# Fused attention, gated MoE and soft-MoE kernel: the last block and the tail of TensorE in written order, serial stages in column halves, six more weight tiles

## The chip, the cores and the metric

The kernel is one program on one core of one Trainium2 chip. The metric is the device time of one execution in microseconds; the figure for the kernel is the median of several runs. A profile is one more execution, taken with the hardware profiler; its span runs from the first to the last instruction of the core.

## The reference

Three parts, each fed by the one before. Sizes: 8 x 8 heads of 576 tokens by 64; 4608 tokens of width 512; a feed-forward width of 2048; 8 experts with 4 slots each and an inner width of 1024.

```python
# chunked attention, chunks of 64 tokens (q_c, k_c, v_c: the inputs cut into chunks)
scores = scale * np.matmul(q_c, k_c.transpose(0, 1, 2, 4, 3))
attn = softmax over the last axis of scores
x = np.matmul(attn, v_c)                    # as 4608 x 512
# gated layer
h = x @ w_in
g = h * (1.0 / (1.0 + np.exp(-1.702 * h)))
x = g @ w_out
# soft mixture of experts, 32 slots
logits = x @ phi
d = np.exp(logits - logits.max(0, keepdims=True)); d /= d.sum(0, keepdims=True) + 1e-09
slot_input = (d.T @ x).reshape(E, S_per_e, D)
for e in range(E):
    slot_out[e] = np.maximum(slot_input[e] @ w1[e], 0.0) @ w2[e]
c = np.exp(logits - logits.max(1, keepdims=True)); c /= c.sum(1, keepdims=True) + 1e-09
out = c @ slot_out.reshape(n_slots, D)
```

(The softmax is written in one line here; the reference subtracts the maximum and divides by the sum with 1e-9 added.)

## The kernel before

**Blocks.** The 4608 tokens are 12 blocks of 384. In a block the gated layer runs over 16 column tiles `f` of 128 columns of the inner width. `gemm` does one of them: twelve full-width matmuls (`h`, lines 324 to 326; the fp32 product is put together from high and low parts), a tanh on ScalarE, and on VectorE the product that gives the gate tile `gt`. `x @ w_out` is never formed: `logits` multiplies the gates by `wp`, a product of `w_out` and `phi` made ahead, in quarter-width matmuls (32 of the 128 columns of the array each) for four column tiles at a time, and `dispatch` sums the gates into the 32 slots (`dtg`, 12 quarter-width matmuls of 512 columns, added to `acc`). The softmax over the tokens is carried from block to block (`slots_a`, factor `cr`), that over the slots stands in `slots_b`. What `dispatch` needs of the gates is their transpose. The other blocks get it by way of DMA; in the last block `gemm_t` transposes on TensorE, three 128x128 transposes per column tile into an accumulator tile `gtp`, copied out by VectorE or ScalarE (`EVAC` says which), one column behind `gemm`. The work of the block before (its last logits `l3`, `slots_a` as `s0`, `slots_b` as `s1`, its `dispatch` as `d0`) and the logits of the last block itself (`l0` to `l2`) are hung on columns by the list `LAST`.

**The tail.** Behind the last column come the last logits, the softmax (`slots_a`), and a chain on TensorE: `dtg` for the last block; four transposes of `acc` (`accp`), copied by ScalarE to `ac`; 16 quarter-width matmuls with `w_out` (`sip`), scaled by VectorE to `si`; four matmuls with the selection matrix `sel` that transpose and sum (`sitp`), spread by VectorE into `sxt`. Then eight up steps `(g, a)`: 32 quarter-width matmuls or more with `w1` (`h1p`), a ReLU on ScalarE (`h1`), two transposes (`htp`), a copy by VectorE (`ht`). Then the down stage for each half `d` of the 512 output columns: for each half `g` of the experts 32 matmuls with `w2` (`fp`), a copy by ScalarE (`f`), and a matmul that sums over experts (`so`). `combine` multiplies by the slot softmax and stores, the first half on the queue of GpSimd (POOL), the second on that of SyncE (SP).

**Order.** Up to the block before the last all engines run in the order in which the code is written. For the last block and the tail only SP does (line 900); there a scheduler puts the instructions of the other engines in order by their dependences and its own estimate.

**Loads of expert weights.** `w1` and `w2` lie packed in one array and are read in the order of use. `load(kind, eng)` fills one tile of a pool: `w`, `s`, `q`, `v`, `x` and `p` are kinds of tile, and `ROOM` says how many 128 KB pieces one holds. `TABLE` hangs loads on columns of blocks 9 to 11 and on three places of the tail (`a`, `b`, `e`); `used` issues a load into a tile when its pieces have been multiplied. These loads are issued on POOL's queue (line 599).

## Time and profile before

| | |
|---|---|
| median of 3 runs | 648.03 us (647.84 to 648.07) |
| the profiled execution | 645.9 us, span 644.1 us, 15618 instructions |
| TensorE busy | 617.8 us, 96% of the span |
| VectorE busy | 450.6 us, 70% |
| ScalarE busy | 233.2 us, 36% |
| GpSimd busy | 68.2 us, 11% |
| moved by DMA | 167.95 MB, mean 261 GB/s |

The profiled execution took 1.8 us more than its span. Busy shares are means over the whole span, and the ends of matmuls are modelled; what a stretch is bound by is read from its own rows.

### The profile page before, as it was taken

Reading aid. Unit: us, or ns where it says so; the run is one execution under the profiler, and the core shown is the slowest. Engines: PE = TensorE matmul, PEld = TensorE weight load, DVE = VectorE, ACT = ScalarE, POOL = GpSimd, SP = SyncE. Lnnn points to the kernel's source line nnn. Section 1 sums busy time; section 2 is a strip of 40 time slices with the busy share of each in tenths; the row PEclk is TensorE's granted clock in tenths of the full one; section 3 lists DMA queues with packets and bytes.
Section 4 is the critical chain, followed back from the end, with each engine's and each line's share of the span. In section 5 each row is a group of like instructions: output and inputs, shape, how many; then the busy total and the mean of one; then the engine's idle time right before and its main releaser. Section 6 shows DMA issues by size and latency. Waiting matters only on the chain.

```text
span 644.1 us, 15618 instructions
## 1 busy us (share of the span) xinstructions
PE 617.8 (96%) x6476; PEld 525.1 (82%) x6476; DVE 450.6 (70%) x981; ACT 233.2 (36%) x481; POOL 68.2 (11%) x101
## 2 busy tenths in 40 slices
PE   8899999999999999999999999999999999978893
PEld 7699887897898798989889989989898898826552
DVE  5899889788697787786886886877857646331033
ACT  4876454342232343333324333433333222121132
POOL 1000010101010010000000010100001111232310
PEclk9999999999999999999999999999999999999997
DMA  8964885559799794785774966956748789889997
GB/s 338 358 197 192 272 283 167 133 156 337 191 346 285 236 341 138 219 306 165 259 258 147 338 200 169 371 136 200 267 122 285 240 285 380 305 297 415 406 395 297
DMA packets 64503, 167.95 MB, mean 261 GB/s; under 512 B 11888, under 2 KB 34544, under 8 KB 64432
## 3 DMA queue, kind: packets, MB, share of 16 engines
q1 hardware_dynamic: 55824, 129.72, 60.6%
q0 software_dynamic: 8608, 37.23, 15.2%
q8 instruction: 51, 0.84, 0.5%
q14 instruction: 20, 0.16, 0.1%
HBM read 122.29 MB, written 44.63 MB: 259 GB/s over the span
## 4 chain that ended last, share of the span: by engine, by line
PE 91%; DVE 4%; ACT 2%; issue 1%; POOL 0%; DVEq 0%; ACTq 0%; POOLq 0%
PE h L324 21%; PE h L326 20%; PE h L325 20%; PE lp L390 5%; PE dtg L526 5%; PE sx L248 3%; PE sx L299 3%; PE pt L284 2%; PE fp L708 2%; PE h1p L688 2%; PE op L737 1%; PE wpp L200 1%; PE gtp L375 1%; PE sip L652 1%; PE htp L697 1%
## 5 line engine op out<-in xcount | busy, mean ns | idle before, releaser
L324 PE MATMUL h<-xh,w 128*128 128x384 f32 x768 | 265.6, 346 | 0.5 <-ACT xh L314 0.5
L326 PE MATMUL h<-xh,w 128*128 128x384 f32 x768 | 257.6, 335 | 0.5 <-DVE w L187 0.5
L325 PE MATMUL h<-xl,w 128*128 128x384 f32 x768 | 257.3, 335 | 0.0
L328 ACT ACTIVATE gt<-h 128x384 f32<-128x384 f32 x192 | 94.0, 490 | 211.8 <-PE h L326 211.6
L324 PEld LDWEIGHTS h<-xh,w 128*128 128x128 f32 x768 | 144.2, 188 | 20.9 <-issue 16.7
L329 DVE SCALAR_TENSOR_TENSOR gt<-gt,h 128x384 f32<-128x384 f32 x192 | 104.8, 546 | 71.3 <-ACT gt L328 70.9
L326 PEld LDWEIGHTS h<-xh,w 128*128 128x128 f32 x768 | 144.1, 188 | 1.6 <-issue 0.8
L325 PEld LDWEIGHTS h<-xl,w 128*128 128x128 f32 x768 | 144.4, 188 | 0.3 <-DVE xl L315 0.3
L339 DVE STREAM_TRANSPOSE g<-gt 128x384 f32<-128x384 f32 x176 | 100.4, 574 | 7.7 <-PE dtg L526 2.3
L273 POOL TENSOR_TENSOR e<-e,rs 128x512 f32<-128x512 f32 x33 | 34.5, 1046 | 459.3 <-DVE rs L272 418.8
L314 ACT ACTIVATE xh<-sx 128x512 fp32r<-128x512 f32 (+1 forms) x38 | 21.7, 576 | 88.0 <-DVE e L260 76.3
L315 DVE TENSOR_TENSOR xl<-sx,xh 128x512 fp32r<-128x512 f32 (+1 forms) x38 | 24.8, 657 | 20.0 <-ACT xh L314 18.6
L599 POOL DMA_DIRECT2D w<-in_moe_w_dram x56 | 29.8, 534 | 84.1 <-PE h L326 36.8
L390 PE MATMUL lp<-gt,wp 128*32 128x384 f32 x384 | 37.0, 492 | 0.1
L526 PE MATMUL dtg<-g,dt 128*32 128x512 f32 x288 | 33.2, 593 | 1.4 <-DVE dt L485 1.4
L259 DVE TENSOR_REDUCE mx<-sx 128x8 f32<-128x512 f32 (+1 forms) x37 | 23.8, 643 | 6.1 <-PE sx L248 6.1
L260 DVE TENSOR_TENSOR e<-sx,mx 128x512 f32<-128x512 f32 (+1 forms) x37 | 25.0, 677 | 2.3 <-DVE mx L259 0.5
L746 DVE COPY o<-op 128x512 f32<-128x512 f32 (+1 forms) x20 | 11.1, 626 | 21.3 <-PE op L737 21.3
L267 ACT ACTIVATE e<-e 128x512 f32<-128x512 f32 x36 | 22.6, 628 | 7.9 <-DVE e L260 7.8
L526 PEld LDWEIGHTS dtg<-g,dt 128*32 128x32 f32 x288 | 8.9, 110 | 19.8 <-issue 18.2
L269 DVE TENSOR_REDUCE sm<-e 128x8 f32<-128x512 f32 x36 | 23.5, 654 | 0.1
L248 PEld LDWEIGHTS sx<-qk 64*64 64x64 f32 x960 | 16.7, 134 | 7.7 <-issue 7.4
(121 smaller groups left out, 551.0 us busy)
## 6 DMA issues: line engine op xcount, KB each, us to landing
g_dram<-g SPq DMA_DIRECT2D x176, 192.0 KB
g<-g_dram SPq DMA_DIRECT2D x44, 768.0 KB
w<-in_moe_w_dram POOLq DMA_DIRECT2D x34, 512.0 KB, 8.9
qk<-in_qk_dram SPq DMA_DIRECT2D x30, 512.0 KB
w<-in_moe_w_dram POOLq DMA_DIRECT2D x17, 768.0 KB, 7.7
stg<-in_moe_w_in_dram SPq DMA_DIRECT2D x16, 512.0 KB
stg<-in_moe_w_out_t_dram SPq DMA_DIRECT2D x16, 512.0 KB
wo<-in_moe_w_out_dram SPq DMA_DIRECT2D x16, 512.0 KB
```

Of the source, the lines that this page charges most:

```text
L248: nc.tensor.matmul(out=y[h][w, hp, :], lhsT=t[r, 0, hp, w], rhs=t[r, 1, hp, w], start=True, stop=True)
L260: nc.vector.tensor_tensor(out=ev[:, hs], in0=v, in1=mx[:, hs].to_broadcast(list(v.shape)), op=ALU.subtract)
L273: (nc.gpsimd if pool else nc.vector).tensor_tensor(out=e, in0=e, in1=rs.to_broadcast([128, 2 * KD, 64]), op=ALU.mult)
L324: nc.tensor.matmul(out=h, lhsT=a, rhs=xh[b][:, k, :], start=(k == 0), stop=False)
L325: nc.tensor.matmul(out=h, lhsT=a, rhs=xl[b][:, k, :], start=False, stop=False)
L326: nc.tensor.matmul(out=h, lhsT=l, rhs=xh[b][:, k, :], start=False, stop=(k == KD - 1))
L328: nc.scalar.activation(out=t, in_=h, func=ACTF.Tanh, scale=0.851)
L329: nc.vector.scalar_tensor_tensor(out=t, in0=t, scalar=1.0, in1=h, op0=ALU.add, op1=ALU.mult)
L339: nc.vector.transpose(out=g1[b, q][:, :, :, 32 * j:32 * (j + 1)], in_=t.rearrange("p (a b c) -> p b a c", b=4, c=32))
L390: nc.tensor.matmul(out=lp[b][32 * j:32 * (j + 1), :], lhsT=wp[:, f, :], rhs=gt[b, f], start=(g == 0), stop=(g == NG - 1),)
L526: nc.tensor.matmul(out=p[32 * j:32 * (j + 1)], lhsT=dt[:, i, :], rhs=g[j][i], start=(i == 0), stop=(i == NCP - 1))
L599: eng.dma_start(out=t[:, 0:at], in_=w12[:, w_at[0]:w_at[0] + at])
```

## The change

`manual_schedule` now holds TensorE too, so that from the last block on it runs in the order of the code. The code is written for that order: `gemm_t` runs two columns behind `gemm` instead of one (its accumulator tiles come from another pool, tags `x` and `s`), the second group of logits moves from column 12 to column 8, and ScalarE and VectorE change places in the copies of columns 14 and 15. In the tail, `dtg`, `accp`, `sip` and `sitp` are done in halves of 256 columns. An up step (`up`) and its transposes (`turn`) are apart: those of a step are written behind the matmuls of the next. In the down stage (`down`, `total`) the sum of the first half of the experts is written in the middle of the second half's matmuls, and the last step's transposes amid the first `fp`. `slots_b` moves behind `sitp`. The 16 blocks of `w_out` are converted in another order (`wo_use`), so that those which `sip` needs first are neighbours. Six loads of a new kind `m` (tiles of the pool that holds gates and ReLU outputs, two pieces of 128 KB each) are hung on columns 10 to 15 of the last block.

```diff
-ROOM = {'w': 4, 's': 6, 'q': 4, 'v': 2, 'x': 2, 'p': 6}
+ROOM = {'w': 4, 's': 6, 'q': 4, 'v': 2, 'x': 2, 'p': 6, 'm': 2}
 TABLE = {'9.15': 'wxx', '10.6': 'q', '10.11': 'vq', '10.15': 'v', '11.0': 'ssw', '11.8': 'sss', 'a': 'ss', 'b': 'ssss', 'e': 'pppppp'}
 TABLE.update({f'11.{f}': TABLE.get(f'11.{f}', '') + 'w' for f in range(1, 16)})
-EVAC = 'vvvvvvvvvvvvvvaa'
-LAST = (('g0', 2), ('l3', 4), ('l0', 4), ('s0', 5), ('s1', 7), ('d0', 9), ('l1', 12), ('l2', 12))
+TABLE.update({f'11.{f}': TABLE[f'11.{f}'] + 'm' for f in range(10, 16)})
+EVAC = 'vvvvvvvvvvvvvvav'
+LAST = (('g0', 2), ('l3', 4), ('l0', 4), ('s0', 5), ('s1', 7), ('d0', 9), ('l1', 8), ('l2', 12))
...
-        if f % 2:
-            p = ps_x[0].tile([128, NCP, 4, 32], F32, tag="x", name="gtp")
-        else:
-            p = ps.tile([128, NCP, 4, 32], F32, tag="pt", name="gtp")
+        p = ps_x[0].tile([128, NCP, 4, 32], F32, tag="x" if f % 2 else "s", name="gtp")
...
+    wo_use = [j * 4 + g for g in range(4) for j in range(4)]
 
     def load_wo(i):
         if i < NF:
...
+    def m_alloc(shape, dtype, name):
         return mid_tile(shape, name, dtype)
...
+        gemm_t(b, NF - 2)
         logits(b, NG - 1)
         gemm_t(b, NF - 1, gt_last)
...
-        dispatch(b)
-        at("b")
+        dt, cr = dt_t.pop(b)
+        gs = g2.pop(b)
...
+        halves = [(h, slice(256 * h, 256 * h + 256), slice(2 * h, 2 * h + 2)) for h in range(2)]
+        for h, cs, fs in halves:
+            p = ps_h.tile([128, 2, 128], F32, tag="h", name="dtg")
+            for i in range(NCP):
+                for j in reversed(range(4)):
+                    nc.tensor.matmul(
+                        out=p[32 * j:32 * (j + 1)], lhsT=dt[:, i, :], rhs=gs[j][i][:, fs, :],
+                        start=(i == 0), stop=(i == NCP - 1),
+                    )
+            nc.vector.scalar_tensor_tensor(
+                out=acc[:, cs], in0=acc[:, cs], scalar=cr, in1=p.rearrange("p f c -> p (f c)"), op0=ALU.mult, op1=ALU.add
+            )
+        at("b")
+        s = stat[b][1]
+        sip = [ps.tile([128, 256], F32, tag="pt", name="sip"), ps_x[0].tile([128, 256], F32, tag="s", name="sip")]
+        acs = []
+        for h, cs, fs in halves:
+            p = (ps_h if h else ps).tile([128, 2, 4, 32], F32, tag="h" if h else "m", name="accp")
+            for z in range(2):
+                nc.tensor.transpose(
+                    p[:, z].rearrange("p g s -> p (g s)"), acc[:, cs][:, 128 * z:128 * (z + 1)], ident
+                )
+            ac = mid_tile([128, 2, 4, 32], "ac")
+            nc.scalar.activation(out=ac, in_=p, func=ACTF.Copy)
+            acs.append(ac)
+        sums = ps.tile([128, 1], F32, tag="lp", name="sums")
+        nc.tensor.matmul(out=sums, lhsT=sel_all, rhs=s, start=True, stop=True)
+        rs = st_p.tile([128, 1], F32, tag="rsum", name="rsum")
+        nc.vector.scalar_tensor_tensor(out=s, in0=stat[b - 1][1], scalar=cr, in1=sums, op0=ALU.mult, op1=ALU.add)
...
+        sx = []
+        for z in range(2):
+            for h, cs, fs in halves:
+                for g in (2 * z, 2 * z + 1):
+                    for j in range(4):
+                        nc.tensor.matmul(
+                            out=sip[h][32 * j:32 * (j + 1), :], lhsT=acs[z][:, g % 2, j, :], rhs=wo_t[j * 4 + g][:, cs],
+                            start=(g == 0), stop=(g == 3),
+                        )
+        at("e")
+        for h, cs, fs in halves:
+            si = mid_tile([128, 256], "si")
+            nc.vector.tensor_scalar(out=si, in0=sip[h], scalar1=rs, scalar2=0.5, op0=ALU.mult, op1=ALU.mult)
+            p = (ps if h else ps_x[0]).tile([128, 2, NS], F32, tag="m" if h else "x", name="sitp")
+            for k in range(2):
+                nc.tensor.matmul(
+                    out=p[:, k, :], lhsT=si[:, 128 * k:128 * (k + 1)], rhs=sel_all[:, 0:32], start=True, stop=True
+                )
+            x = sxt[h]
+            y = p.rearrange("p k (e i) -> p k e i", i=4)
+            nc.vector.tensor_copy(x[:, :, 0:252].rearrange("p k (e x) -> p k e x", x=36)[:, :, :, 0:4], y[:, :, 0:7])
+            nc.vector.tensor_copy(x[:, :, 252:256], y[:, :, 7])
+            sx += [x[:, 0, :], x[:, 1, :]]
         slots_b(b)
         load_ct(slice(NT // 512 - 1, NT // 512))
...
+        ht, h1 = {}, {}
+
+        def up(g, a):
+            n = 2
...
+            used(*[(1, 4 * g + j, a + z) for j in range(4) for z in range(n)])
+            h1[g, a] = mid_tile([128, n, 128], "h1")
+            nc.scalar.activation(out=h1[g, a], in_=p, func=ACTF.Relu)
+
+        def turn(g, a):
+            n, v = 2, h1.pop((g, a))
+            p = ps.tile([128, n, 128], F32, tag="m", name="htp")
+            if a % 4 == 0:
+                ht[g, "t"] = mid_tile([128, 4, 128], "ht")
+            t = ht[g, "t"]
+            for c in range(n):
+                nc.tensor.transpose(p[:, c, :], v[:, c, :], ident)
+                ht[g, a + c] = t[:, (a + c) % 4, :]
+            nc.vector.tensor_copy(t[:, a % 4:a % 4 + n, :], p)
+
+        steps = [(g, a) for g in range(2) for a in range(0, KE, 2)]
+        for i, x in enumerate(steps):
+            up(*x)
+            if i:
+                turn(*steps[i - 1])
+        so, fp = {}, {}
+
+        def down(d, g, ks):
+            if 0 in ks:
+                fp[d, g] = ps.tile([128, DH], F32, tag="lp" if g else "pt", name="fp")
+            p = fp[d, g]
+            for k in ks:
                 for j in range(4):
-                    c, i = a, 0
-                    while c < a + n:
...
+                    nc.tensor.matmul(
+                        out=p[32 * j:32 * (j + 1), :], lhsT=ht[g, k][:, 32 * j:32 * (j + 1)],
+                        rhs=w2_t[d, 4 * g + j, k], start=(k == 0), stop=(k == KE - 1),
+                    )
...
+            if KE - 1 in ks:
+                f = fp[d, g] = mid_tile([128, DH], "f2")
+                nc.scalar.activation(out=f, in_=p, func=ACTF.Copy)
+
+        def total(d, g):
+            if g == 0:
+                so[d] = ps_x[0].tile([128, DH], F32, tag="x", name="so")
+            nc.tensor.matmul(out=so[d], lhsT=sel_all, rhs=fp.pop((d, g)), start=(g == 0), stop=(g == 1))
+
         for d in range(2):
-            so = ps_x[0].tile([128, DH], F32, tag="x", name="so")
-            for g in range(2):
-                p = ps.tile([128, DH], F32, tag="pt", name="fp")
-                for k in range(KE):
-                    for j in range(4):
-                        nc.tensor.matmul(
-                            out=p[32 * j:32 * (j + 1), :], lhsT=ht[g, k][:, 32 * j:32 * (j + 1)],
-                            rhs=w2_t[d, 4 * g + j, k], start=(k == 0), stop=(k == KE - 1),
-                        )
-                    if k % 4 == 3:
-                        used(*[(2, d, 4 * g + j, k - z) for j in range(4) for z in range(4)])
-                f = mid_tile([128, DH], "f2")
-                nc.scalar.activation(out=f, in_=p, func=ACTF.Copy)
-                nc.tensor.matmul(out=so, lhsT=sel_all, rhs=f, start=(g == 0), stop=(g == 1))
+            down(d, 0, range(4))
+            if d == 0:
+                turn(*steps[-1])
+            down(d, 0, range(4, KE))
+            down(d, 1, range(4))
+            total(d, 0)
+            down(d, 1, range(4, KE))
+            total(d, 1)
             sr = mid_tile([128, DH], "sr")
-            nc.scalar.activation(out=sr, in_=so, func=ACTF.Copy)
+            nc.scalar.activation(out=sr, in_=so[d], func=ACTF.Copy)
             combine(d, sr)
 
...
-            if b == NB - 1 and f:
-                gemm_t(b, f - 1)
+            if b == NB - 1 and f > 1:
+                gemm_t(b, f - 2)
...
-        with tc.manual_schedule(engines={SP}):
+        with tc.manual_schedule(engines={SP, PE}):
             with tc.tile_pool(name="ps_t", bufs=1, space=bass.MemoryType.PSUM) as ps_x[0]:
                 block(NB - 1)
                 tail()
```

The order of instructions on each engine shows what the written order does at two places. The first is TensorE in the last block, behind column 4. `lp_6350` is the last logits group of the block before, the other `lp` is the first group of the last block, `gt_...` are gates (of columns 0 to 3 where `lp` is theirs), `gtp_...` their transposes, and `h_...` with `xh_6336` and `xl_6337` the matmuls of column 5. TensorE before:

```order
L390 MATMUL lp_6350<-gt_6674,wp_89 32x384
L390 MATMUL lp_6816<-gt_6705,wp_89 32x384
L390 MATMUL lp_6816<-gt_6727,wp_89 32x384
L390 MATMUL lp_6816<-gt_6751,wp_89 32x384
L390 MATMUL lp_6816<-gt_6782,wp_89 32x384
L375 MATMUL gtp_6821<-ident_87,gt_6782 128x128 x3
L324 MATMUL h_6828<-xh_6336,w_530 128x384
L375 MATMUL gtp_6731<-ident_87,gt_6705 128x128 x3
L325 MATMUL h_6828<-xl_6337,w_530 128x384
```

The transposes of columns 3 and 0 stand here with matmuls of column 5 between them. TensorE after:

```order
L388 MATMUL lp_6350<-gt_6674,wp_89 32x384
L388 MATMUL lp_6811<-gt_6705,wp_89 32x384
L388 MATMUL lp_6811<-gt_6727,wp_89 32x384
L388 MATMUL lp_6811<-gt_6745,wp_89 32x384
L388 MATMUL lp_6811<-gt_6777,wp_89 32x384
L373 MATMUL gtp_6816<-ident_87,gt_6745 128x128 x3
L325 MATMUL h_6823<-xh_6336,w_530 128x384
L326 MATMUL h_6823<-xl_6337,w_530 128x384
```

Now it is the transposes of column 2, and the matmuls of column 5 follow. Columns 0 and 1 have been transposed earlier.

VectorE at the same place; `lps1` is the subtraction that makes the low part of the block before's logits, and `gtp_6762` (before) and `gtp_6757` (after) are read by the copies of columns 1 and 0. Before:

```order
L379 COPY g2_0_6730<-gtp_6762 128x12x32
L329 SCALAR_TENSOR_TENSOR gt_6751<-gt_6751,h_6738 128x384
L329 SCALAR_TENSOR_TENSOR gt_6782<-gt_6782,h_6769 128x384
L329 SCALAR_TENSOR_TENSOR gt_6805<-gt_6805,h_6792 128x384
L405 TENSOR_TENSOR lps1_6813<-lp_6350,lps0_6812 128x384
L379 COPY g2_0_6730<-gtp_6821 128x12x32
L379 COPY g2_0_6730<-gtp_6731 128x12x32
L379 COPY g2_0_6730<-gtp_6785 128x12x32
```

One of the copies stands ahead of three gates and `lps1`, three behind. After:

```order
L330 SCALAR_TENSOR_TENSOR gt_6777<-gt_6777,h_6764 128x384
L330 SCALAR_TENSOR_TENSOR gt_6800<-gt_6800,h_6787 128x384
L403 TENSOR_TENSOR lps1_6808<-lp_6350,lps0_6807 128x384
L377 COPY g2_0_6756<-gtp_6757 128x12x32
L377 COPY g2_0_6756<-gtp_6780 128x12x32
L377 COPY g2_0_6756<-gtp_6816 128x12x32
```

All three copies stand behind `lps1`, and the first of them, of `gtp_6757`, empties the tile that `gtp_6816` writes on TensorE.

The second place is TensorE in the up steps; `h1p_...` are the matmuls of steps, `h1_7348` (before) and `h1_7388` (after) the ReLU of a step, `htp_...` its transposes. Before:

```order
L688 MATMUL h1p_7319<-w12_6683,sxt_7210 32x128
L688 MATMUL h1p_7319<-w12_6710,sxt_7210 32x128
L688 MATMUL h1p_7354<-w12_6712,sxt_7209 32x256
L688 MATMUL h1p_7354<-w12_6736,sxt_7209 32x256
L688 MATMUL h1p_7354<-w12_6767,sxt_7209 32x256
L697 MATMUL htp_7350<-ident_87,h1_7348 128x128 x2
```

The transposes stand behind three matmuls of the next step. After:

```order
L710 MATMUL h1p_7395<-w12_6785,sxt_7200 32x256
L710 MATMUL h1p_7395<-w12_6712,sxt_7200 32x256
L710 MATMUL h1p_7395<-w12_6730,sxt_7200 32x256
L710 MATMUL h1p_7395<-w12_6762,sxt_7200 32x256
L710 MATMUL h1p_7395<-w12_6785,sxt_7200 32x256
L725 MATMUL htp_7422<-ident_87,h1_7388 128x128 x2
```

They stand behind the last matmul of the next step (`h1p_7395`), ahead of the one after that.

## Rows read from the trace of the kernel before

**Rows 1.** Busy us by stretch: PE, PEld, DVE, ACT, POOL, granted clock, DMA share, GB/s

```profile
549.00:560.00 11.00, 11.00 (x76) 9.64 (x75) 4.82 (x10) 1.97 (x4) 2.83 (x6) 1.00 0.90 340
560.00:571.00 11.00, 9.45 (x70) 5.29 (x68) 4.42 (x15) 3.23 (x9) 2.09 (x4) 1.00 0.83 288
571.00:573.50 2.50, 1.47 (x14) 0.72 (x6) 1.22 (x5) 0.36 (x1) 1.19 (x3) 1.00 0.37 43
573.50:615.00 41.50, 35.94 (x610) 22.63 (x612) 6.80 (x21) 6.34 (x16) 14.14 (x27) 1.00 1.01 403
...
628.00:631.00 3.00, 3.00 (x50) 2.30 (x46) 2.14 (x4) 2.06 (x4) 0.00 (x0) 1.00 0.07 22
```

**Rows 2.** Timeline of PE, serial stages: start, us, instruction [wait ahead, releaser]

```profile
568.72 2.78 PE L526 MATMUL dtg<-g,dt 128*32 128x512 f32 x24 [1.38 <-DVE dt L485]
...
572.45 0.66 PE L637 MATMUL accp<-ident,acc 128*128 128x128 f32 x4 [0.64 <-DVE acc L532]
573.79 3.64 PE L652 MATMUL sip<-wo,ac 128*32 128x512 f32 x32 [0.69 <-ACT ac L639]
578.38 1.08 PE L661 MATMUL sitp<-sel,si 128*128 128x32 f32 x8 [0.95 <-DVE si L658]
579.74 0.40 PE L688 MATMUL h1p<-w,sxt 128*32 128x256 f32 x1 [0.28 <-DVE sxt L668]
```

**Rows 3.** Waits of PE, 579 to 628 us: total us, times, longest

```profile
PE htp L697 <- ACT h L694: 2.0, 6, 0.5
```

**Rows 4.** Timeline of PE, down stage

```profile
605.62 0.70 PE L716 MATMUL so<-f,sel 128*128 128x256 f32 x2 [0.53 <-ACT f L715]
...
621.67 0.70 PE L716 MATMUL so<-f,sel 128*128 128x256 f32 x2 [0.56 <-ACT f L715]
622.30 3.66 PE L708 MATMUL fp<-w,ht 128*32 128x256 f32 x64
```

**Rows 5.** Timeline of DVE, last block

```profile
530.59 0.56 DVE L405 TENSOR_TENSOR lps<-lp,lps 128x384 fp32r<-128x384 f32 x1 [0.26 <-ACT lps L404]
531.16 1.18 DVE L379 COPY g<-gtp 128x384 f32<-128x384 f32 x2
...
564.10 0.55 DVE L329 SCALAR_TENSOR_TENSOR gt<-gt,h 128x384 f32<-128x384 f32 x1 [1.59 <-ACT gt L328]
```

**Rows 6.** Timeline of PE, last block

```profile
530.58 0.55 PE L375 MATMUL gtp<-ident,gt 128*128 128x128 f32 x3
...
560.61 0.33 PE L325 MATMUL h<-xl,w 128*128 128x384 f32 x1
560.79 0.34 PE L326 MATMUL h<-xh,w 128*128 128x384 f32 x1
...
561.47 0.34 PE L325 MATMUL h<-xl,w 128*128 128x384 f32 x1
...
563.38 0.49 PE L375 MATMUL gtp<-ident,gt 128*128 128x128 f32 x3
```

**Rows 7.** Groups by line, 563 to 645 us: busy us, mean ns, idle before

```profile
L532 DVE SCALAR_TENSOR_TENSOR acc<-acc,cr,dtg 128x512 f32<-128x512 f32 x1 | 0.7, 749 | 0.6 <-PE dtg L526 0.6
...
L701 DVE COPY ht<-htp 128x256 f32<-128x256 f32 x8 | 3.4, 425 | 18.3 <-PE htp L697 18.3
...
L694 ACT ACTIVATE h<-h1p 128x256 f32<-128x256 f32 x8 | 3.1, 384 | 24.2 <-PE h1p L688 24.2
```

**Rows 8.** Timeline of PE, up steps

```profile
585.16 1.93 PE L688 MATMUL h1p<-w,sxt 128*32 128x256 f32 x32
587.55 0.44 PE L697 MATMUL htp<-ident,h 128*128 128x128 f32 x2 [0.46 <-ACT h L694]
587.92 1.93 PE L688 MATMUL h1p<-w,sxt 128*32 128x256 f32 x32
```

**Rows 9.** Timeline of POOL: the last load of weights is issued

```profile
608.50 0.54 POOL L599 DMA_DIRECT2D w<-in_moe_w_dram  x1 [0.75 <-DMA w<-in_moe_w_dram]
```

**Rows 10.** DMA issues, 608 to 609.5 us: KB, us from issue to landing

```profile
w<-in_moe_w_dram POOLq DMA_DIRECT2D x1, 256.0 KB, 8.9
```

91 lines of the change are left out of this document (25 added, 66 removed).

## Prediction, made before the changed kernel was run

> **What bounds the kernel now.** I read the busy time by stretch first. From 549 us to 571 us TensorE has hardly a free moment while matmuls of the last block run (11.00 of 11.00 us, then 9.45 of 11.00), so nothing that only hides work there can pay; it pays to take work or waits off TensorE. The same view shows the DMA side: its engines are busy 0.90, 0.83 and 0.37 of the three stretches up to 573.5 us, then 1.01 of a stretch of 41.5 us while the expert weights stream in, and idle (0.07) from 628 to 631 us [rows 1]. The tail is therefore a chain through TensorE beside a full stream of loads, and both have to be followed. The chain of waits and the timeline of TensorE give the chain: four serial stages from 568.72 us to 579.74 us with waits of 0.64, 0.69, 0.95 and 0.28 us on VectorE and ScalarE [rows 2]; eight up steps, each followed by two transposes that wait for the ReLU on ScalarE, 2.0 us in all [rows 3]; and in the down stage sums that wait for a copy by ScalarE [rows 4]. The time behind 628 us is stores.
>
> **The change, part by part.**
>
> *Last block, in written order.* Four things move. (a) The order shows that the transposes of column 2 now stand directly behind eight logits matmuls. They write the accumulator tile that column 0 wrote, which must first be copied out, and on VectorE that copy stands behind the subtraction `lps1`. In the trace before, that subtraction starts at 530.59 us, and the two copies behind it start at 531.16 us and take 1.18 us, so the first ends at about 531.75 us [rows 5]; TensorE came to the place behind the logits at 530.58 us [rows 6]. Before, TensorE had other work whose tile was free. Now it stands: +1.2 us, and behind it in its queue wait the matmuls of column 5, so everything later moves. (b) The logits of columns 4 to 7 are a group of their own, at column 8. The matmuls are the same, but there is one change more from full-width to quarter-width work and back. A change costs about 0.15 us (worked out below): +0.3 us. (c) The transposes of column 13 leave the full stretch and go behind the last matmul of column 15, where TensorE waits for that column's gate anyway. Two matmuls that start 0.17 us apart without transposes start with three of them between at 560.79 us and, two matmuls on, at 561.47 us, so the three cost 0.68 - 0.35 = 0.33 us: -0.3 us. (d) VectorE copies them out before it finishes the gate of column 15. Transposes that start at 563.38 us take 0.49 us [rows 6], a copy 0.56 us (half of the 1.18 us less a little), so VectorE would be free at about 564.4 us; it began the gate at 564.10 us [rows 5]: +0.3 us. Together +1.5 us at 568.72 us. The bounds of (a) are 0 us (the copy comes sooner) and 1.8 us (both copies are waited for).
>
> *Serial stages in halves.* The waits sum to 0.64 + 0.69 + 0.95 + 0.28 = 2.56 us [rows 2]. A copy of 256 columns takes VectorE 0.43 us against 0.75 us for 512, ScalarE 0.38 us [rows 7]. First half: its accumulation on VectorE (0.43 us) lies under the second half of `dtg` (half of 2.78 us). The second half's lies only under the first two transposes (half of 0.66 us), so with 0.15 us of hand-over about 0.25 us stays. ScalarE's first copy (0.38 us) lies under the other two transposes and that wait. The first `si` lies under the last quarter of `sip` (0.9 us), the second under the first half of `sitp` (0.5 us), and the first `sxt` copies under its second half. I keep another 0.2 us for hand-overs. 2.56 - 0.45 = 2.1 us: -2.1 us, bounds 1.5 and 2.5 us. The normalising work of `slots_b` moves behind; on VectorE it stands between the two accumulations in about 0.5 us where the second half is not ready yet, so it costs nothing; without that cover it would cost these 0.5 us.
>
> *Up steps.* Before, the 16 matmuls from 587.92 us are preceded by transposes that started at 587.55 us after 0.46 us of waiting; the period from the matmuls at 585.16 us is 2.76 us [rows 8]. Now the transposes of a step are written behind the whole next step, whose 1.93 us hide the ReLU (0.38 us) [rows 7]. What goes is the waiting, 2.0 us by the view of waits [rows 3]: -2.0 us, bounds 1.6 and 3 us. What does not go is the change between the two kinds of work: matmuls follow 0.37 us after the start of two transposes [rows 8], and two transposes themselves cost 2 x 0.11 = 0.22 us by the 0.33 us for three, so 0.15 us is the change. There are as many of them as before. The Trainium skill, "TensorEngine Tiling (Array Packing)", section Tiling Modes, says that changing the tiling mode drains TensorE. The row agrees (0.15 us). By that rule a sum made from streaming time alone would promise too much: 16 changes of 0.15 us, 2.4 us more.
>
> *Down stage.* The sum of the first half of the slots is now written amid the second half's matmuls, so its wait of 0.53 us in the first pass and 0.56 us in the second goes [rows 4]; those of the second halves stay, since nothing is left to put there: -1.1 us, bounds 0.9 and 1.4 us.
>
> *Loads.* Six loads of 256 KB are issued from column 10 on, behind a load of 512 KB each. They carry 1.57 MB, 3.9 us at the 403 GB/s of the full stretch. Up to 573.5 us the engines are idle for 0.10 x 11 + 0.17 x 11 + 0.63 x 2.5 = 4.5 us [rows 1], so they fit into it, and the stream behind has 3.9 us less to bring. It starts 1.5 us later, with the last block: 2.4 us earlier at its end. The chain does not live on this, since the last load is issued at 608.50 us [rows 9] and lands 8.9 us on [rows 10], at 617.4 us, while the last pass that needs such data starts at 622.30 us [rows 4]; it covers the tail's gain. The stores of the first half end at about 628 - 2.4 = 625.6 us, and those of the second would start at 631 - 3.7 = 627.3 us: no collision, 1.7 us to spare. The order of the `w_out` blocks changes no bytes: 0. The six tiles come out of the pool that also holds the gates and the ReLU outputs; their old contents are last read several columns earlier, so I count no wait.
>
> Sum: +1.5 - 2.1 - 2.0 - 1.1 = -3.7 us, made against a span of 644.1 us (645.9 us with what lies around it). The median of the runs is 648.03 us, 2.1 us above that execution; the same 3.7 us off it gives **644.3 us**.
>
> **The rivals.**
>
> *The changes of mode are hidden too.* If TensorE could begin transposes under the tail of quarter-width matmuls once nothing has to be waited for, the 2.4 us above would go as well: -6.1 us, 641.9 us. Against it: the 0.15 us stands also where nothing was waited for [rows 8].
>
> *The stores bound the end.* If the six loads only push others back, the stream is not 2.4 us earlier but 1.5 us later. First-half stores then end at 629.5 us, second-half ones start there instead of at 631 us, and only 1.5 us come out: 646.5 us. For it: the engines are already busy 0.9 and 0.83 of the time there [rows 1]. Against it: the idle time exceeds the need. The Trainium skill, "DMA: Bandwidth & Descriptors", section Anatomy of one DMA, gives 2.0 us plus bytes by 436 GB/s for each DMA; done one by one the six would take an estimated 15.6 us by that page, more than the idle time. The trace has several loads in flight, so I do not take it so.
>
> *Slower: the wait of (a) recurs.* In written order TensorE can only stand where the scheduler slipped other matmuls in. If copies ran late at every column, 13 more sets of transposes would wait; an average above (3.7 / 13 =) 0.28 us each turns the sign, and 0.56 us each, a whole copy, gives +3.6 us, 651.6 us. Against it: VectorE is busy 4.82 of 11.00 us there [rows 1], and only at column 4 do logits, subtraction and two copies meet.
>
> *It does nothing*: the written order hides what the scheduler already hid, within 0.2% of 648.0 us. Against it: the waits stand in the rows.
>
> **How the numbers follow.** My forecast 0.60 (its own range 642.7 to 645.9 us, from the bounds of the terms), hidden changes 0.17, stores 0.12, slower 0.06, nothing 0.05. The range 641.6 to 646.6 us takes in the forecast, the stores and most of the hidden changes, and leaves out about 0.2. A measurement of this kernel can tell 0.2% (1.3 us) from no change; faster by more than that 0.87, within it 0.07, slower 0.06.
>
> **What would show it.** In the profile after, a wait of about 1.2 us of TensorE for VectorE's copy in the last block, and none at other columns; 9 us from `dtg` to the first up step instead of 11.02; no wait of the ReLU's transposes and a period near 2.3 us in the up steps; one wait before a sum for each half of the columns instead of two; the DMA engines hardly idle before 574 us. The forecast is wrong if waits for weights appear in the down stage, if the stores of both halves run into each other, or if the last block loses more than 2 us.

## Result and the profile after

The changed kernel takes 640.77 us (median of 4 runs, 639.26 to 641.21) against 647.93 us before (4 runs, 645.62 to 648.07): a ratio of 0.9894, interval 0.9866 to 0.9921. Timed a second time it gave 0.9893 (0.9871 to 0.9914). It is faster, as forecast, but by 7.2 us (1.1%) instead of 3.7, and 0.8 us below the range. The profiled execution took 639.26 us with a span of 637.5 us, 6.6 us less than the span before.

Where the time went is read best by stages. All kernels here run the same code up to the sum of block 9 (the `dtg` matmuls of that block). Its first matmul starts at 509.26 us in the trace before and at 508.96 us in the one after; over all traces of this study it lies between 508.64 and 511.24 us. So I count from there, and this spread is no part of any comparison. The ends are those of the spans, which are given to 0.1 us. From that matmul to the first `dtg` of the last block, on to the first up step (`h1p`), to the first output matmul (`op`) of the first half, to that of the second half, and to the end of the span:

| us | to last `dtg` | to `h1p` | to `op`, first half | to `op`, second half | to the end | sum |
|---|---|---|---|---|---|---|
| before | 59.46 | 11.02 | 32.18 | 15.78 | 16.40 | 134.84 |
| after | 60.27 | 8.82 | 27.61 | 15.09 | 16.75 | 128.54 |
| difference | +0.81 | -2.20 | -4.57 | -0.69 | +0.35 | -6.30 |
| predicted | +1.5 | -2.1 | -2.55 | -0.55 | 0 | -3.7 |

The view of waits of the changed kernel, TensorE, 515 to 645 us (total us, times, longest):

```profile
PE dtg L642 <- DVE dt L483: 1.4, 1, 1.4
PE gtp L373 <- DVE g L377: 1.1, 1, 1.1
PE so L755 <- ACT f L750: 1.1, 2, 0.6
PE op L786 <- ACT sr L767: 0.9, 2, 0.5
PE accp L656 <- DVE acc L646: 0.3, 1, 0.3
```

The waits of the ReLU's transposes [rows 3] and those ahead of `sip`, `sitp` and `h1p` [rows 2] are gone, two of the four sums wait, and one new wait of 1.1 us for a copy by VectorE stands there. All of this was forecast, down to the place of the new wait. The sizes are what has to be explained. (In the views PE is TensorE, PEld its loads of the stationary operand, DVE VectorE, ACT ScalarE. A quarter-width matmul of the code stands in the trace as two, and counts of matmuls below are those of the trace.) The timeline of TensorE in the changed kernel shows the stages:

```profile
529.18 1.50 PE L388 MATMUL lp<-gt,wp 128*32 128x384 f32 x16
531.79 0.52 PE L373 MATMUL gtp<-ident,gt 128*128 128x128 f32 x3 [1.11 <-DVE g L377]
...
572.71 0.44 PE L656 MATMUL accp<-ident,acc 128*128 128x128 f32 x2 [0.31 <-DVE acc L646]
572.98 0.28 PE L663 MATMUL sums<-sum,sel 128*128 128x1 f32 x2
573.19 3.66 PE L673 MATMUL sip<-wo,ac 128*32 128x256 f32 x64
576.78 1.33 PE L683 MATMUL sitp<-sel,si 128*128 128x32 f32 x8
578.04 0.40 PE L710 MATMUL h1p<-w,sxt 128*32 128x256 f32 x1
...
582.02 1.93 PE L710 MATMUL h1p<-w,sxt 128*32 128x256 f32 x32
583.89 0.44 PE L725 MATMUL htp<-ident,h 128*128 128x128 f32 x2
584.26 1.93 PE L710 MATMUL h1p<-w,sxt 128*32 128x256 f32 x32
586.12 0.44 PE L725 MATMUL htp<-ident,h 128*128 128x128 f32 x2
...
595.53 1.93 PE L742 MATMUL fp<-w,ht 128*32 128x256 f32 x32
597.40 0.44 PE L725 MATMUL htp<-ident,h 128*128 128x128 f32 x2
...
604.48 0.70 PE L755 MATMUL so<-f,sel 128*128 128x256 f32 x2 [0.56 <-ACT f L750]
605.66 5.60 PE L786 MATMUL op<-sr,ct 32*128 32x256 f32 x72 [0.47 <-ACT sr L767]
```

An up step has a period of 2.24 us (582.02 to 584.26) instead of 2.76 [rows 8]. Look at the row of 582.02 us: its modelled end is 582.02 + 1.93 = 583.95 us, but the transposes start at 583.89 us, 0.06 us ahead of it. Before, the same row ended at 587.09 us and the transposes started 0.46 us behind that [rows 8]; the gain of the step is 2.39 - 1.87 = 0.52 us, more than the wait that the view lists.

Busy time by stretch in the changed kernel (columns as in [rows 1]):

```profile
560.00:571.00 11.00, 9.51 (x86) 6.26 (x88) 5.25 (x16) 2.86 (x8) 3.47 (x7) 1.00 0.96 358
571.00:573.50 2.50, 2.19 (x34) 1.27 (x30) 1.43 (x5) 0.70 (x2) 0.94 (x2) 1.00 0.46 184
573.50:575.00 1.50, 1.50 (x36) 0.91 (x32) 0.33 (x3) 0.06 (x1) 1.17 (x3) 1.00 0.67 132
575.00:615.00 40.00, 38.89 (x704) 26.28 (x700) 10.48 (x24) 9.11 (x22) 14.90 (x28) 1.00 1.02 411
615.00:623.00 8.00, 7.02 (x104) 4.04 (x94) 1.09 (x2) 2.12 (x6) 0.00 (x0) 1.00 1.02 424
623.00:626.00 3.00, 3.00 (x40) 2.02 (x36) 3.00 (x6) 2.85 (x7) 0.00 (x0) 1.00 0.89 362
626.00:635.00 9.00, 0.34 (x4) 0.00 (x0) 1.45 (x4) 0.89 (x3) 0.00 (x0) 0.66 1.01 419
```

The six loads filled the stretch up to 571 us (0.96 instead of 0.83 busy). From 575 us the DMA engines are full, with a dip to 0.89 at 623 to 626 us, until the last store. The idle 3 us between the stores of the two halves [rows 1] are gone. By the packets in the trace, the second half's stores now start (624.11 us) while the first half's still run (to 624.93 us); before they started 1.4 us behind them. That goes with the 0.35 us given back at the end: where the two do not meet and no packets lag (before, and in runs 1, 3 and 8 below), the last packet starts 14.91 to 14.94 us after the second half's first output matmul, and here 15.28 us after it, in the second trace of this kernel 15.20 us.

### The profile page after: what moved, and what is told of

It reads as the page before. It is cut to its first block, busy times and chain, and to the rows that moved or that the text cites. A ratio compares the mean times of both kernels' runs of the same rounds, so it can differ in the third digit from the quotient of the medians.

```text
span 637.5 us, 15724 instructions
## 1 busy us (share of the span) xinstructions
PE 615.6 (97%) x6524; PEld 526.3 (83%) x6524; DVE 451.4 (71%) x980; ACT 233.0 (37%) x481; POOL 69.9 (11%) x104
## 4 chain that ended last, share of the span: by engine, by line
PE 93%; DVE 3%; ACT 2%; issue 1%; POOL 0%; DVEq 0%; POOLq 0%; ACTq 0%
PE h L325 22%; PE h L327 21%; PE h L326 21%; PE lp L388 5%; PE dtg L524 5%; PE sx L249 3%; PE sx L300 3%; PE pt L285 2%; PE h1p L710 2%; PE fp L742 2%; PE op L786 1%; PE gtp L373 1%; PE wpp L201 1%; PE sip L673 1%; PE lg L411 1%
## 5 line engine op out<-in xcount | busy, mean ns | idle before, releaser
L601 POOL DMA_DIRECT2D w<-in_moe_w_dram x59 | 31.6, 537 | 79.5 <-PE h L327 33.0
L524 PE MATMUL dtg<-g,dt 128*32 128x512 f32 x264 | 30.4, 593 | 0.0
L131 ACT ACTIVATE stg<-stg 128x512 f32<-128x512 f32 x32 | 21.5, 673 | 3.5 <-DMA stg<-in_moe_w_out_t_dram 2.9
```

The lines of the kernel that those rows point to most:

```text
L524: nc.tensor.matmul(out=p[32 * j:32 * (j + 1)], lhsT=dt[:, i, :], rhs=g[j][i], start=(i == 0), stop=(i == NCP - 1))
L601: eng.dma_start(out=t[:, 0:at], in_=w12[:, w_at[0]:w_at[0] + at])
```

## Experiments

The same stages for every kernel that was run, with the ratio of its times to the kernel before:

| us | to last `dtg` | to `h1p` | to `op` 1 | to `op` 2 | to the end | sum | ratio (95%) |
|---|---|---|---|---|---|---|---|
| changed kernel again | 60.25 | 8.82 | 27.57 | 15.08 | 16.64 | 128.36 | 0.9893 (0.9871 to 0.9914) |
| 1 transposes directly behind | 60.26 | 8.82 | 32.87 | 15.09 | 16.39 | 133.43 | 0.9983 (0.9966 to 1.0) |
| 2 serial stages in one piece | 60.26 | 10.97 | 28.20 | 15.08 | 18.27 | 132.78 | 0.9966 (0.9951 to 0.9982) |
| 3 sums directly behind | 60.25 | 8.82 | 28.13 | 15.66 | 16.42 | 129.28 | 0.9922 (0.9905 to 0.994) |
| 4 last block as before | 60.27 | 8.82 | 27.56 | 15.08 | 16.48 | 128.21 | 0.9897 (0.9878 to 0.9916) |
| 5 without the six loads | 60.25 | 8.82 | 27.83 | 15.61 | 20.15 | 132.66 | 0.995 (0.9931 to 0.9969) |
| 6 VectorE in written order | 60.01 | 9.58 | 27.56 | 15.09 | 17.37 | 129.61 | 0.9913 (0.9893 to 0.9933) |
| 7 as 4, column 15 by VectorE | 59.45 | 8.82 | 27.61 | 15.09 | 17.52 | 128.49 | 0.9891 (0.9864 to 0.9918) |
| 8 two loads more | 60.38 | 8.89 | 27.50 | 15.09 | 16.40 | 128.26 | 0.9886 (0.9864 to 0.9909) |
| 9 both 7 and 8 | 59.54 | 8.89 | 27.50 | 15.08 | 16.67 | 127.68 | 0.9881 (0.986 to 0.9902) |
| 10 as 9, second half begun earlier | 59.58 | 8.89 | 29.98 | 12.19 | 17.95 | 128.59 | 0.9902 (0.9881 to 0.9922) |
| 11 before, with the six loads | 60.30 | 12.63 | 33.90 | 15.66 | 17.10 | 139.59 | 1.0044 (1.0027 to 1.006) |

**The changed kernel again**, without an edit.

> The changed kernel itself once more, for the spread between executions: so far the part that no kernel here changes (up to the sum of block 9) took 508.6 to 511.2 us. From that sum to the end the changed kernel took 128.5 us; it should do so again within 0.5 us, and the ratio to the kernel before should be near 0.989.

It repeats to 0.2 us in the sum and 0.1 us in each stage, while its part ahead of the sum of block 9 took 1.9 us more (510.84 us). So by this one pair stages can be compared to about 0.2 us, whole times only to 0.2%. The last column is an exception: in runs 2, 6, 7 and 10 a few of the last packets of the stores come 1 to 2 us behind the rest. Where this matters I also give the start of the 850th of the 864 packets of the second half's stores, counted from the sum of block 9. It is 133.20 us before the change and 126.64 and 126.50 us in the two traces of the changed kernel.

**1. Transposes directly behind their step.**

```diff
             up(*x)
-            if i:
-                turn(*steps[i - 1])
+            turn(*x)
...
             down(d, 0, range(4))
-            if d == 0:
-                turn(*steps[-1])
```

> The changed kernel with the two transposes of each up step written directly behind the step's own matmuls again; all else as changed. Theory now: in the changed kernel transposes start 0.31 us (256-wide matmuls) or 0.20 us (128-wide) after the start of the last matmul ahead of them; waiting for the ReLU they start 0.83 or 0.72 us after it. The difference is 0.52 us for each of the 8 steps whether the view of waits shows a wait there or not: TensorE comes to the first output matmuls 4.2 us later (605.7 to about 609.9 us), the span goes from 637.5 to about 641.3 us, since the stores had held the end up by 0.35 us. The prediction's reading (only the waits that the view of waits lists, 2.0 us in all, were there to be won): 2.0 us later, span about 639.2 us.

5.26 us came back on TensorE, 0.66 us for each step: far from the 2.0 us of the prediction and over the 4.2 us of the theory. The timeline of TensorE in this kernel:

```profile
585.79 1.93 PE L710 MATMUL h1p<-w,sxt 128*32 128x256 f32 x32
588.30 0.44 PE L725 MATMUL htp<-ident,h 128*128 128x128 f32 x2 [0.58 <-ACT h L716]
588.68 1.93 PE L710 MATMUL h1p<-w,sxt 128*32 128x256 f32 x32
591.25 0.44 PE L725 MATMUL htp<-ident,h 128*128 128x128 f32 x2 [0.64 <-ACT h L716]
```

The listed waits sum to 4.8 us here, since nothing at all stands between a step and its transposes; in the kernel before, the scheduler had put matmuls of the next step there (three, at the step whose order is shown). Taken from the starts of single matmuls, the eight gaps between the last matmul ahead of the transposes and the transposes sum to 4.93 us before, 1.95 us after and 7.19 us here. 7.19 - 1.95 = 5.24 us, which is the stage's whole 5.26 us. So the stage follows this sum, and the list of waits (4.8 us) misses 0.4 us of it. The theory's mechanism holds; its 0.83 us for the gap came from the order of before and was too small for this one.

**2. Serial stages in one piece.** `dtg`, `accp`, the copy, `sip`, `si` and `sitp` over 512 columns as before the change, in the written order of after.

```diff
-        for h, cs, fs in halves:
-            p = ps_h.tile([128, 2, 128], F32, tag="h", name="dtg")
+        p = ps.tile([128, 512], F32, tag="m", name="dtg")
...
-            si = mid_tile([128, 256], "si")
-            nc.vector.tensor_scalar(out=si, in0=sip[h], scalar1=rs, scalar2=0.5, op0=ALU.mult, op1=ALU.mult)
+        si = mid_tile([128, 512], "si")
+        nc.vector.tensor_scalar(out=si, in0=sip, scalar1=rs, scalar2=0.5, op0=ALU.mult, op1=ALU.mult)
```

> The changed kernel with the serial stages (sum of gates into slots, transposes of the sum, the product with w_out, its transposes) in one piece of 512 columns each, in written order. If the halves hide the copies, as predicted and as the times from the first sum matmul to the first up step say (11.02 us before, 8.82 us after), that stretch goes back to about 11.0 us, and the span rises by 1.9 us or so to 639.4 us. Rival: the order alone hid them (normalising moved behind, sums moved behind the transposes); then the stretch stays under 9.4 us and the span under 638 us.

The stretch is back at 10.97 us: the halves do it, not the order. This kernel also lost 0.6 us on the way to the first output and 1.5 us at the end, which the edit does not explain. The 0.6 us are one interval, between the first two matmuls of the first `fp` (597.90 to 598.54 us). The 1.5 us are late packets: the 850th starts 14.86 us after the second half's first output matmul, as in the changed kernel, and the last 1.9 us behind it. Why is open; the ratio says that some of the loss was in the timed runs too.

**3. Sums directly behind the matmuls that they sum.**

```diff
             down(d, 0, range(4, KE))
+            total(d, 0)
             down(d, 1, range(4))
-            total(d, 0)
             down(d, 1, range(4, KE))
```

> The changed kernel with the first sum over experts of each output half directly behind the matmuls that it sums, as before the change. The prediction's reading: two waits of 0.53 and 0.56 us come back, 1.1 us in all, span about 638.3 us. Theory now (a gap is counted from the start of the last matmul, not from its modelled end): the down stages were 1.04 and 0.69 us shorter after the change, so 1.5 to 1.7 us come back, span about 638.8 us.

0.56 us and 0.58 us come back against the changed kernel's second trace, 1.1 us together: the prediction's term for the sums was right. The 2 us that the down stages gained must hold something else (below).

**4. The last block as before the change**, the tail as changed.

```diff
-('l1', 8), ('l2', 12))
+('l1', 12), ('l2', 12))
...
-            if b == NB - 1 and f > 1:
-                gemm_t(b, f - 2)
+            if b == NB - 1 and f:
+                gemm_t(b, f - 1)
...
-        with tc.manual_schedule(engines={SP, PE}):
-            with tc.tile_pool(name="ps_t", bufs=1, space=bass.MemoryType.PSUM) as ps_x[0]:
+        with tc.tile_pool(name="ps_t", bufs=1, space=bass.MemoryType.PSUM) as ps_x[0]:
+            with tc.manual_schedule(engines={SP}):
                 block(NB - 1)
+            with tc.manual_schedule(engines={SP, PE}):
                 tail()
```

> The changed kernel with the last block as before the change (transposes one column behind, logits in the old groups, its instructions on TensorE ordered by the scheduler), the six loads and the whole tail as changed. The prediction's reading: the written order costs 1.5 us there, so the tail's first sum matmul comes 1.5 us earlier (569.2 to 567.7 us). Theory now: of the 1.2 us wait and the extra logits group some 0.7 us are paid for by gaps of the scheduler's order (0.34 us of a wait for a copy, and transposes set into the middle of a column), so it comes 0.8 us earlier (568.4 us); the span falls by as much if the loads behind the sum move with it (636.7 us), and stays near 637.5 us if the stores cannot follow.

Nothing moved, which is neither answer. The timeline of TensorE shows a wait that neither kernel had:

```profile
565.86 0.55 PE L376 MATMUL gtp<-ident,gt 128*128 128x128 f32 x3
567.37 0.91 PE L459 MATMUL lg<-lps,sel 128*128 128x384 f32 x2 [0.96 <-ACT lps L399]
```

ScalarE, still ordered by the scheduler, now copies column 15's transposes ahead of the last logits, and TensorE waits for the logits. Up to the last column the block ran like the one before the change; the 0.8 us were lost behind it. Run 7 repeats it without this wait.

**5. Without the six loads.**

```diff
-TABLE.update({f'11.{f}': TABLE[f'11.{f}'] + 'm' for f in range(10, 16)})
```

> The changed kernel without the six loads of 256 KB from column 10 on; the same bytes then come in later loads. Theory now: in the changed kernel the stores end the run, since the DMA engines are full from 575 us until the last store (635.7 us) without a gap. Without the six loads 1.57 MB (3.9 us at 403 GB/s) move into that full stretch, TensorE keeps its times, the first-half stores end some 3.5 us later and the second-half ones with them: span about 641 us (+3.5). The prediction's reading (the chain on TensorE bounds the end and the stores have 1.7 us to spare): 3.9 - 1.7 = 2.2 us at most, span 639.7 us or less. Rival: weights come late instead; then waits for weights appear on TensorE in the second half of the down stage, where the last load lands 4.0 us ahead of its use now.

The sum grows by 4.1 us: 0.7 us on TensorE, 3.4 us behind the first output matmul of the second half. Stretches of this kernel:

```profile
573.00:576.00 3.00, 2.69 (x42) 1.57 (x38) 1.84 (x8) 0.77 (x2) 0.90 (x2) 1.00 0.09 23
576.00:577.00 1.00, 1.00 (x26) 0.57 (x22) 0.16 (x1) 0.00 (x0) 1.00 (x3) 1.00 0.90 201
577.00:617.00 40.00, 38.89 (x708) 26.18 (x704) 10.48 (x24) 9.02 (x21) 15.14 (x30) 1.00 1.02 404
617.00:628.00 11.00, 9.99 (x138) 5.83 (x132) 3.09 (x6) 4.16 (x9) 1.49 (x3) 1.00 1.02 420
628.00:640.00 12.00, 1.35 (x16) 0.64 (x10) 2.45 (x5) 1.78 (x5) 0.00 (x0) 0.65 1.02 425
```

The DMA engines are idle for 3 us and then full from 577 to 640 us. The second half's stores start 5.7 us after its first output matmul instead of 3.4, while the first half's are still being moved, and their 850th packet comes 3.85 us later than in the changed kernel (130.49 us). That is the 3.5 us of the theory rather than the 2.2 us of the prediction's reading: with TensorE 3 us earlier than predicted, hardly anything is left to spare. The rival came true in small, since in the second half's last 32 matmuls TensorE does wait for weights once:

```profile
620.12 1.43 PEld L741 LDWEIGHTS fp<-w,ht 128*32 128x32 f32 x26 [0.36 <-DMA w<-in_moe_w_dram]
```

They take 0.5 us longer than in the changed kernel. The other 0.2 us on TensorE are eight more matmuls of the up steps (376 as before the change, since the tiles are cut otherwise).

**6. VectorE, too, in written order.**

```diff
-        with tc.manual_schedule(engines={SP, PE}):
+        with tc.manual_schedule(engines={SP, PE, mybir.EngineType.DVE}):
```

> The changed kernel with VectorE, too, in written order in the last block and the tail. There the copy of column 0's transposes stands ahead of the subtraction instead of behind it. If this order alone makes the 1.1 us wait of TensorE behind the eight logits matmuls, the wait goes and the tail's first sum matmul comes 1.2 us earlier (60.3 to 59.1 us after the first sum matmul of the block before); the loads that wait for it move along, so the span falls by about 1.2 us. Rival: the subtraction's data are late and VectorE, in written order, stands in other places instead (the softmax of the block before has six dependent steps with ScalarE there); then gates come later and the gain is under 0.5 us.

The rival. The wait behind the logits is gone, so VectorE's order did make it, but the timeline of TensorE has two new ones:

```profile
540.85 0.55 PE L373 MATMUL gtp<-ident,gt 128*128 128x128 f32 x3 [0.96 <-DVE g L377]
...
579.44 0.60 PE L683 MATMUL sitp<-sel,si 128*128 128x32 f32 x4 [0.86 <-DVE si L680]
```

At 540.85 us a copy stands behind the softmax of the block before, at 579.44 us the second `si` behind the spreading of the first `sitp`. 0.26 us were won ahead of the last `dtg` and 0.76 us lost behind it. (In the 17.37 us at the end the last packet comes 1.15 us behind the 850th, in the changed kernel 0.4 us.)

**7. Run 4, mended:** column 15 is copied by VectorE, column 14 by ScalarE, as in the changed kernel.

> The earlier run with the last block as before, mended: there ScalarE copied column 15's transposes ahead of the logits, so TensorE waited 1.0 us for them. Now VectorE copies column 15 as in the changed kernel. Theory now: the written order of the last block costs 0.8 us of TensorE against the scheduler's, so the tail's first sum matmul comes 59.5 us after that of the block before instead of 60.3 us. The prediction's reading: 1.5 us, so 58.8 us.

59.45 us: the written order of the last block costs 0.8 us, not 1.5. The scheduler's order has losses of its own, which the timeline of TensorE in this kernel shows (it is the order before the change):

```profile
542.23 0.33 PE L327 MATMUL h<-xh,w 128*128 128x384 f32 x1
542.40 0.34 PE L325 MATMUL h<-xh,w 128*128 128x384 f32 x1
542.91 0.55 PE L376 MATMUL gtp<-ident,gt 128*128 128x128 f32 x3 [0.17 <-DVE g L380]
543.21 0.42 PE L326 MATMUL h<-xl,w 128*128 128x384 f32 x1
543.47 0.49 PE L376 MATMUL gtp<-ident,gt 128*128 128x128 f32 x3
```

The transposes at 542.91 us start 0.51 us behind the matmul ahead of them, where 0.17 us is the usual step; those at 543.47 us start 0.26 us behind a single matmul. Of the 0.8 us that TensorE was earlier, the end shows 0.05 us, but the stores do show it: their 850th packet starts at 125.82 us, 0.7 to 0.8 us earlier than in the changed kernel. Only the last packets came late in this execution, with the DMA engines nearly idle (share 0.07):

```profile
636.00:637.00 1.00, 0.00 (x0) 0.00 (x0) 0.00 (x0) 0.00 (x0) 0.00 (x0) 0.50 0.07 31
```

Runs 9 and 10 go on from here.

**8. Two loads more**, issued behind the last column.

```diff
-'a': 'ss',
+'a': 'ssmm',
```

> The changed kernel with two more loads of 256 KB, issued behind the last column, where the DMA engines are partly idle from 572 to 575 us. If the stores end the run only by the 0.35 us that the second-half stores start late, the stream ends 1.3 us earlier and the span falls by no more than 0.35 us. If the stream bounds the end altogether, the span falls by 1.3 us. Rival: the two tiles are missed by the tail's own small tiles, and TensorE waits for ScalarE or VectorE in the serial stages; then the span rises.

The end comes 0.35 us sooner after the second half's first output matmul (16.40 us, as in the kernel before), 0.28 us in the sum, but only 0.1 us against the changed kernel's second trace, and the 850th packet starts at 126.62 us, as without the edit. The last load lands 0.6 us earlier, not 1.3. An earlier stream gives at most the 0.35 us of the collision of the stores; for the rest TensorE bounds the end. With run 5, where a later stream did move it, the two bound the end to within about 0.4 us of each other.

**9. Both 7 and 8.**

> The last block as before with column 15 copied by VectorE (TensorE 0.8 us earlier, the end was not) together with the two more loads (stream 1.3 us earlier, TensorE not; the end 0.3 us earlier). If the end waits for the later of TensorE and the stream of loads and stores, as the theory now says, both together give what neither gave alone: 128.5 - 0.8 - 0.3 = 127.4 us from the sum of block 9 to the end. Rival: what the stores gave back in the former run was chance in the last stores; then the two add up from 128.5 and 128.3 us to 128.2 us or so.

127.68 us, nearer to the theory's 127.4 than to the rival's 128.2. But the packets speak for the rival's reason: the 850th starts at 125.80 us, against 125.82 in run 7 alone and 126.62 in run 8 alone. So the last block's 0.8 us had reached the stores in run 7 already, where late packets hid it, and the two loads add nothing. That both are needed is not shown. The timed ratio, 0.9881 against 0.9893, does not separate this kernel from the changed one.

**10. The second half begun earlier.**

```diff
...
+        down(0, 1, hi)
+        down(1, 0, lo)
+        total(0, 1)
+        sr = out_rows(0)
+        down(1, 0, hi)
+        combine(0, sr)
...
```

> The former kernel, and in the down stage the first matmuls of the second output half are written ahead of the second sum of the first half and of its product with the slot softmax, so that their waits (0.94 - 0.31 us and 0.85 - 0.3 us between starts) are covered too. TensorE then comes to the second half's stores 1.2 us earlier. Theory now (the stream of loads and stores bounds the end): the stream is full from 575 us on and has at most 0.5 us to give, so the end moves by 0 to 0.5 us, 126.9 to 127.4 us from the sum of block 9. Rival (TensorE bounds the end): 126.2 us.

TensorE came to the second half's output 0.4 us earlier, not 1.2 (a new wait of 0.5 us for the copy out of a tile of the first half's output), and the end later by 0.9 us than in run 9. The first half's stores were issued 2.5 us later, and the DMA engines, done with the weights, were only 0.63 to 0.89 busy from 611 to 613 us, 0.5 us of idle time in sum, where they were full in run 9. No gain came of TensorE alone, as the theory said: the 850th packet starts at 125.74 us, 0.06 us earlier than in run 9. That the edit costs 0.9 us is not shown, since it lies in the packets behind the 850th (the last starts at 127.12 us, in run 9 at 126.24 us).

**11. The kernel before with the six loads alone.**

```diff
+TABLE.update({f'11.{f}': TABLE[f'11.{f}'] + 'm' for f in range(10, 16)})
...
```

> The kernel before with the six loads of 256 KB on columns 10 to 15 of the last block and nothing else of the change. Theory now: there TensorE bounds the end and the DMA engines stand idle for 3 us between the stores of the two halves, so an earlier stream brings nothing: the last load lands 2 to 3.5 us earlier, the first-half stores end as much earlier, and from the sum of block 9 to the end it still takes 134.8 us (within 0.3 us). Rival: the loads are a part of the gain by themselves, 2 us or more, 132.8 us or less. Other rival: the tiles that they take make the tail's copies wait, over 135.3 us.

Slower: 139.59 us, and 1.0044 in the timed runs, above the expected 134.8 us and the 135.3 us from which the other rival speaks. The last load did land earlier, by 1.6 us (2 to 3.5 had been expected), and it brought nothing: the DMA engines then stood idle until the first half's stores. What cost time is TensorE, 4.0 us later at the second half, so the run does not price the loads by themselves. The timeline of TensorE and the stretches:

```profile
567.52 0.91 PE L459 MATMUL lg<-lps,sel 128*128 128x384 f32 x2 [0.96 <-ACT lps L399]
568.36 0.37 PE L472 MATMUL lq<-lps,sel 128*32 128x96 f32 x8
570.11 4.38 PE L527 MATMUL dtg<-g,dt 128*32 128x512 f32 x24 [1.38 <-DVE dt L486]
```

```profile
569.00:570.00 1.00, 0.00 (x0) 0.00 (x0) 0.41 (x4) 0.61 (x3) 0.00 (x0) 0.98 0.79 270
570.00:571.00 1.00, 0.89 (x8) 0.24 (x12) 0.73 (x4) 0.17 (x1) 0.00 (x0) 0.50 0.98 344
571.00:572.00 1.00, 1.00 (x12) 0.34 (x8) 0.75 (x4) 0.12 (x1) 0.00 (x0) 0.50 0.96 381
572.00:573.00 1.00, 1.00 (x12) 0.21 (x7) 0.38 (x2) 0.00 (x0) 0.00 (x0) 0.50 0.65 270
```

With the six loads in the program, ScalarE's copies stand in the order of run 4 (0.96 us of waiting), and behind this wait and the next one the granted clock is 0.50, the lower of its two levels, for some 3 us, and again from 584 to 587 us: the same 24 matmuls take 4.38 us instead of 2.78 [rows 2]. TensorE's further waits up to the first up step are those of the kernel before [rows 2], so no wait for the six tiles themselves shows.

## Why the prediction was too small

**Mechanism.** Every wait that was said to go has gone, the one that was said to come has come at its place with 1.1 us, the serial stages took 8.8 us where 9 had been forecast, and the changes between the two kinds of work have stayed. This last point decides against the rival at 641.9 us, though it came nearest to the measured time: the return from transposes to quarter-width matmuls takes 1.62 us for all eight in the trace before and 1.62 us after. The way there stays as well: with nothing to wait for, transposes start 0.31 us after the last of four 256-column matmuls, where the next four start 0.20 us after it. The Trainium skill, "TensorEngine Tiling (Array Packing)", section Tiling Modes, has TensorE drained at each change of mode. These rows agree in so far as a change costs about 0.1 us each way; a drain as such they cannot show, since the ends of matmuls are modelled. The rivals "nothing" and "slower" fell; the slower one's wait stands at one place only (1.1 us), but run 6 shows that another order of VectorE brings it at others.

**The step that failed: "What goes is the waiting, 2.0 us by the view of waits".** That term measured 3.2 us. From the first up matmul to the last transposes it took 21.34 us before (579.74 to 601.08) and takes 19.36 us after, less 1.56 us between the first and the last of 32 matmuls of the down stage that now lie in it. Of this difference of 3.5 us, 2.98 us are the gaps ahead of the transposes (4.93 to 1.95 us) and 0.23 us the steps' own matmuls (376 before, 368 after, since the tiles are cut otherwise). The remaining 0.3 us are no gain of the steps: they are six matmuls of the down stage that the scheduler had set into the last step.

Of the 2.98 us, 2.0 us are the listed waits. 0.4 us more come with them, because the view counts from the modelled end of the last matmul, and transposes start 0.06 or 0.07 us ahead of that end. 0.3 us were gained at two steps that have no entry in the view (0.42 to 0.21 us and 0.42 to 0.31 us between starts):

```profile
582.24 0.44 PE L697 MATMUL htp<-ident,h 128*128 128x128 f32 x2
584.80 0.44 PE L697 MATMUL htp<-ident,h 128*128 128x128 f32 x2
```

The last 0.2 us are narrower matmuls: at two steps the matmul ahead of the transposes has 128 columns now instead of 256, and they start 0.20 us after it instead of 0.31. Run 1 shows that these gaps are what counts: the stage follows their sum to 0.02 us. The prediction's own bound of 3 us for this term was too low as well.

**Down stage, -1.1 us:** measured -2.05 us (5.26 us for both stages less 3.2). The term for the first sums was sized rightly: 0.91 to 0.31 us and 0.94 to 0.31 us between starts, and run 3 gives 1.1 us back. What had been put at nothing is the rest. The copy ahead of the second sum of the first half came 0.28 us late before and does so no more; its wait was this:

```profile
610.75 0.70 PE L716 MATMUL so<-f,sel 128*128 128x256 f32 x2 [0.84 <-ACT f L715]
```

The second half's second sum gained 0.06 us, and 0.5 us lie between single matmuls of the first half's passes (6.87 us before, 6.39 us after). No run tests these three.

**Last block, +1.5 us:** measured +0.8 us, by difference and by run 7. The wait (a) was right. What was left out is that the order before had losses too, which end when it goes: 0.34 and 0.09 us at the place shown in run 7 and 0.15 us behind column 4, where transposes stand behind a single matmul. Only waits that the change adds had been counted, none of those that it takes away.

**Serial stages, -2.1 us:** -2.2 us, and run 2 gives it back.

**Loads and stores.** That the six loads fit into idle time was right in the main: by the stretches, 1.33 MB more than before were moved between 549 and 573.5 us, of their 1.57 MB, and the last load landed 2.9 us earlier (105.3 us after the sum of block 9 instead of 108.2), where 2.4 had been forecast. "The DMA engines hardly idle before 574 us" did not come: they were 0.46 busy from 571 to 573.5 us. That the chain does not live on the loads fits run 11, which has them alone and shows no gain, and that they cover the tail's gain was right too (run 5: without them 4.1 us of it are lost). "No collision, 1.7 us to spare" failed, as a consequence of the rest: TensorE was 2.9 us earlier than forecast, so the second half's stores met the first half's, which goes with the 0.35 us at the end.

**The sum.** +0.8 - 2.2 - 3.2 - 2.05 + 0.35 = -6.3 us from the sum of block 9, and 0.3 us that the profiled execution was quicker ahead of it, make the 6.6 us of the spans. Three terms were off to the same side: the up steps by 1.2 us, the down stage by 0.95 us, the last block by 0.7 us. With 0.1 us on the serial stages, and less the 0.35 us of the stores, that makes the 2.6 us between -3.7 and -6.3. Taken off the median before as the prediction did it (648.03 us), 6.3 us give 641.7 us, just inside the range. The further 0.9 us of the measured median stand in no stage; executions of the changed kernel spread by twice that (639.26 to 641.21 us).

## What to carry to other kernels

A wait that is removed is worth the interval between the starts of the instructions on both sides of it less the interval that the same pair has where nothing is waited for. The list of waits, counted from modelled ends, was too low here (2.0 us against 2.8), and steps with no entry gained too. When an order is replaced, price the losses of the old order as carefully as those of the new one. And when a chain on TensorE is shortened, follow the stream beside it: in the kernel before, where TensorE bounds the end, the loads alone brought no gain (run 11), and in the changed kernel their absence costs 4 us (run 5), because there both end within about 0.4 us of each other. And look at the last packets before a change of the end is believed: in runs 2, 7 and 10 they came late enough to hide 0.8 us or to feign 0.9 us and more.

## What was not expected of the hardware

The clock: in run 11 a stall of 0.96 us and one of 1.38 us close behind it were followed by a granted clock of 0.50 for about 3 us, which cost 1.6 us on 24 matmuls; in run 4 the same two waits left it at full speed. What made the difference is open. The part of the program that no kernel here changes took between 508.6 and 511.2 us from one execution to another, with the granted clock at 1.00 in each trace, which is as much as the terms that were to be told apart.
